# A long-convolution and expert kernel on one core: the filter's input laid out transposed and its constants loaded early, the experts' two turns joined, and the second to last stores issued from GpSimd's queue

## The chip, the cores and the metric

The kernel runs on 1 core of one Trainium2 chip. The metric is device time in microseconds (us) of one execution; lower is better. Before the change it was run three times: median 2395.51 us, from 2389.8 to 2403.55. One execution more was recorded by the hardware profiler; all trace times below are of that one and count from the start of its span. The engines are PE (matrix multiply; its weight loads are listed apart as PEld), ACT, DVE, POOL (GpSimd) and SP (which here only issues transfers).

## What is computed

Two layers follow each other. The first is a long convolution along the sequence (B = 4, S = 11456, D = 128) with a filter that a small network makes from position embeddings; the second sends each of the 45824 rows to one of E = 8 experts (F = 1024).

```python
h_filt = (np.maximum(pos_emb @ w1, 0.0) @ w2) * np.exp(-0.01 * pos)[:, None]
u = x * v
y = irfft(rfft(u, n=2*S) * rfft(h_filt, n=2*S))[:, :S]      # along the sequence
rows = (x * y).reshape(B * S, D)
...
logits = rows @ w_gate + modality_bias[modality_id]
e_idx = np.argmax(logits, axis=1)
gate_w = softmax(logits)[arange(N), e_idx]
for e in range(E):
    out[e_idx == e] = gate_w * (np.maximum(rows[e_idx == e] @ w1[e], 0.0) @ w2[e])
```

## The kernel before

**The convolution** is a two-stage transform of length 90 x 64, written as matrix products. An outer stage turns the sequence, in NQ = 16 parts, into the SBUF tile `A`, which has two blocks `A[:, 0]` and `A[:, 1]`; a middle stage works through `A` in NG = 30 groups of three rows; the inverse outer stage brings `A` back. The filter goes through the outer and the middle stage once, ahead of the four batches, and uses only `A[:, 0]`. Then every batch is transformed forward, multiplied with the filter's spectrum and transformed back; while a batch is transformed back, its rows are routed to the experts and the next batch is transformed forward.

**The filter's outer stage** (`filter_stages`) takes a part `q` through `load` (256 KB of position embeddings, on SP's queue), `turn` (four PE transposes, one ACT copy), `hidden` (four matmuls with `w1`, then one DVE operation that applies max and the window) and `transform` (four matmuls, two ACT copies into `A`). **Its middle stage** (`filter_middle`) takes a group `g` through `load` (192 KB of constants into a tile `b2`), `turn` (three transposes, an ACT copy `aT`), `spectrum` (three matmuls into `pz`; ACT and DVE split the result into a rounded half and a remainder, stacked as `z`) and `second` (four matmuls with `ws`, the split `w2`; ACT and DVE put the result into a tile `h`, from a ring of three, and POOL's queue stores it to the DRAM tensor `hs`, 384 KB a group).

**The order** on PE, ACT, DVE and SP is the order in which the code is written. Short tables (`FOUT`, `FMID`, `OUTER`, `LAST`, `MID`) give each stage's delay in steps; `steps` turns them into a list of steps, and `overlapped` lays the last F steps of one list over the first F of the next. `F1` lays the filter's middle over its outer stage; `F2` = 2 lays the first batch's forward stage (`load` of `x` and `v`, `product` on DVE, `transform` on PE) over the filter's last two steps. POOL's queue runs in program order too. Tiles named by `new_a` come from one pool of NA = 11 buffers, so that a load waits until the buffer that it is given has been read. A transfer waits besides for the one that was issued eight earlier through the same kind of queue.

**Routing.** For the last batch (`b == nb - 1`) the table `LAST` applies. Each of its NO = 8 parts `o` ends in `store` (the rows with their gate and token number, two transfers to `xr`) and `places` (their places, two transfers to `xi`), both on SP's queue. The very last part's `choice`, `store`, `send` and `places` are kept for `finale` and run inside the expert loop. `fetch` and `send_rows` read `xr` and `xi` back and scatter the rows, by indirect transfers from POOL's queue, into the expert-sorted tensor `xs`.

**The experts** (`experts`) run over 99 tiles of 512 rows, or 256 for the last ones. `rows_in(i)` loads a tile's rows (`x`, four buffers) on SP's queue, and for the first eight tiles their weights too; `rows_turn` transposes them (`px`) and splits them into `xh` and `xl`; `hidden` and `result` are three matmuls each per chunk `c` of 128 hidden units (eight chunks a tile), with `result` two chunks behind; after the last chunk ACT copies the sum to `oT`; `rows_out` transposes that (`pt`), DVE multiplies it by the gate into `ot`, and POOL's queue scatters the rows to `out`. In chunk 5 of a tile stands `rows_turn` of the next tile, in chunk 2 `rows_out` of the tile before.

Of the kernel before, what the change touches and what calls it, by code (L numbers as in the profile page):

```python
# [12 lines left out]
F32 = mybir.dt.float32  # L13
# [24 lines left out]
G = 3  # L38
# [21 lines left out]
FOUT = "load:0 transform:4 turn:1 hidden:2"  # L60
FMID = "turn:2 spectrum:3 second:5 load:1"
MID = "minus:2 turn:1 inverse:5 back:4 load_c:3 spectrum:2 load:0"
GD, OV, EA, MB, EM = 2, 2, 3, 1, 4
F1, F2, F3 = 1, 2, 1
# [113 lines left out]
def hyena_moe_kernel(ctx: ExitStack, tc: tile.TileContext, a: dict, out: bass.AP,  # L178
# [176 lines left out]
    with ExitStack() as cv:  # L355
# [22 lines left out]
        ws = keepp.tile([D, 2, D], F32R, name="ws")  # L378
# [24 lines left out]
        def split_constants():  # L403
            dve.tensor_copy(base, sm("reg"))
            dve.tensor_copy(both, small[:, SMALL["tri"][0]:SMALL["ones"][1]])

            act.copy(ws[:, 0], wf[:, 0])
            dve.tensor_sub(ws[:, 1], wf[:, 0], ws[:, 0].bitcast(F32))
# [78 lines left out]
        def filter_stages():  # L487
# [7 lines left out]
            def turn(q):  # L495
                t = kept.pop((q, "emb"))
                pT = bank("pT")
                for i in range(4):
                    pe.transpose(pT[:, D * i:D * i + D], t[:, D * i:D * i + D], ident)
                pTs = kept[q, 0] = new_a("pTs")[:, 0:512]  # L500
                act.copy(pTs, pT)

            def hidden(q):
                pTs = kept.pop((q, 0))
                m1 = bank("m1")
                for i in range(4):
                    pe.matmul(m1[:, D * i:D * i + D], pTs[:, D * i:D * i + D], wf[:, 1],
# [19 lines left out]
            todo = dict(turn=turn, hidden=hidden, transform=transform, load=load)  # L527
# [5 lines left out]

        def filter_middle():
# [4 lines left out]
            def load(g):  # L539
                t = kept[g, "b"] = new_a("b2")[0:2 * N2, 0:2 * GK].rearrange(  # L540
                    "p (j d) -> p j d", j=G)
                sp.dma_start(t, a["c_bc"][g, :, 0:2 * GK].rearrange("p (j d) -> p j d", j=G))

            def turn(g):
# [3 lines left out]
                aT = kept[g, "aT"] = new_a("aT")[0:2 * N2, 0:G * D]  # L548
                act.copy(aT, pa[0:2 * N2, 0:G * D])

            def spectrum(g):
                aT, b2 = kept.pop((g, "aT")), kept.pop((g, "b"))
                pz = bank("pz")
                zv = pz[:, 0:2 * GK].rearrange("p (m j) -> p m j", j=G)
                for j in range(G):
                    pe.matmul(zv[:, :, j], aT[:, D * j:D * j + D], b2[:, j],
                              start=True, stop=True)
                z = kept[g, "z"] = new_a("z", F32R)[:, 0:4 * GK].rearrange(
                    "p (b m) -> p b m", b=2)

                halves = slice(0, 64), slice(64, D)
                for blk, at in enumerate(halves):
                    act.copy(z[at, blk], pz[at, 0:2 * GK])
                for blk, at in enumerate(halves):
# [624 lines left out]
```

## Time and profile before

| of the profiled execution | |
|---|---|
| its time | 2370.12 us |
| its span, first to last instruction | 2367.9 us |
| granted PE clock, mean over the span | 0.977 |
| median of the three runs beside it | 2395.51 us |
| filter, outer stage: first PE instruction to first of the middle stage | 3.66 to 49.57 us |
| filter, middle stage, to the first product of batch 0 | 49.57 to 118.84 us |
| batch 0 forward, to the first transpose of its middle stage | 118.84 to 163.74 us |
| first expert row tile transposed | 1254.04 us |
| PE busy 1400 to 1500 | 97.27 us |

The times of the profile are read as stretches: which engine is busy in a stretch without a break, and, where it is not, what ended its wait. A row of the timeline has the start, the duration in us, the engine, the line, the operation with its output and inputs, the count of instructions that are merged in it, and in brackets the idle time before it with what ended it.

```profile
PE 2238.2 (95%) x14826; PEld 1874.1 (79%) x14826; DVE 1839.2 (78%) x3197; ACT 1515.7 (64%) x2969; POOL 994.7 (42%) x987
PEclk9999999999899999899998999999999999999999
DMA  3976667677867788575556722112221111111111
```

The first row has each engine's busy time and share of the span; the other two cut the span into 40 slices of 59 us and give, in tenths, the clock granted to PE and the busy share of the 16 transfer engines.

### The profile page before, as it was taken

The numbers are of one execution on the slowest core, as the hardware profiler recorded it, in microseconds if no ns is written. First come the engines' busy times: TensorE is split into PE (matmuls) and PEld (weight loads), VectorE is DVE, ScalarE is ACT, GpSimd is POOL, SyncE is SP. The second block draws the span as 40 slices with busy tenths as digits, with TensorE's granted clock in tenths as the row PEclk, the third lists the DMA queues.
The fourth block names the chain that finished last, engine by engine and source line by source line (L and its number), as shares of the span: only waits on it lengthen the run. The fifth ranks groups of instructions, "written<-read, shape, count | busy, mean of one in ns | idle before, by whom it ended". The sixth has DMA issues, their size and how long they took to land. (4 is left out here: it accounts for less than half of the span.)

```text
span 2367.9 us, 44124 instructions
## 1 busy us (share of the span) xinstructions
PE 2238.2 (95%) x14826; PEld 1874.1 (79%) x14826; DVE 1839.2 (78%) x3197; ACT 1515.7 (64%) x2969; POOL 994.7 (42%) x987
## 2 busy tenths in 40 slices
PE   8899999899989999899888999999999999999998
PEld 8789966798669966698446777777878888888898
DVE  3789888897788978797566777777777877777797
ACT  5757677577556766576445666666666666666676
POOL 0305400376435755276652554445444333333333
PEclk9999999999899999899998999999999999999999
DMA  3976667677867788575556722112221111111111
GB/s 114 314 298 197 220 223 223 185 226 260 288 209 227 225 285 298 183 222 174 174 163 184 246 68 72 61 62 74 67 62 60 59 46 45 45 46 46 39 41 34
DMA packets 188751, 359.04 MB, mean 152 GB/s; under 512 B 33937, under 2 KB 120285, under 8 KB 188521
## 3 DMA queue, kind: packets, MB, share of 16 engines
q1 hardware_dynamic: 161753, 296.77, 39.5%
q0 software_dynamic: 26608, 59.36, 7.4%
q8 instruction: 120, 1.97, 0.3%
q14 instruction: 110, 0.90, 0.1%
q10 hardware_dynamic: 160, 0.03, 0.0%
HBM read 271.63 MB, written 84.83 MB: 151 GB/s over the span
## 5 line engine op out<-in xcount | busy, mean ns | idle before, releaser
L1072 DVE SCALAR_TENSOR_TENSOR hl<-ph,hh 128x512 fp32r<-128x512 f32 x724 | 499.1, 689 | 249.7 <-ACT hh L1071 147.7
L1071 ACT ACTIVATE hh<-ph 128x512 fp32r<-128x512 f32 x724 | 434.0, 600 | 376.1 <-PE ph L1068 232.1
L1108 POOL DMA_INDIRECT out<-ot,idx x362 | 357.8, 988 | 651.3 <-DVE ot L1105 568.1
L264 POOL DMA_INDIRECT xs<-back,to x360 | 379.6, 1054 | 230.6 <-DVE y L701 81.3
L1066 PE MATMUL ph<-xh,wh 128*128 128x512 f32 (+1 forms) x792 | 304.0, 384 | 2.9 <-ACT wh L1037 2.9
L1089 PE MATMUL po<-hh,wh 128*128 128x512 f32 (+1 forms) x792 | 303.5, 383 | 0.0
L1068 PE MATMUL ph<-xl,wh 128*128 128x512 f32 (+1 forms) x792 | 295.7, 373 | 0.1
L1091 PE MATMUL po<-hl,wh 128*128 128x512 f32 (+1 forms) x792 | 294.9, 372 | 0.0
L1067 PE MATMUL ph<-xh,wl 128*128 128x512 f32 (+1 forms) x792 | 294.5, 372 | 0.0
L1090 PE MATMUL po<-hh,wl 128*128 128x512 f32 (+1 forms) x792 | 293.9, 371 | 0.0
L641 POOL TENSOR_TENSOR more<-more 128x384 f32<-128x384 f32 x112 | 112.4, 1004 | 278.0 <-DVE more L638 233.9
L647 DVE TENSOR_TENSOR part<-pz,rings 128x768 f32<-128x768 f32 x240 | 217.6, 948 | 0.0
L664 PE MATMUL pw<-rings,yT 128*128 128x128 f32 x1440 | 184.4, 279 | 5.4 <-DMA rings<-in_c_bc 5.4
L628 PE MATMUL pz<-rings,aT 128*128 128x128 f32 x1440 | 184.4, 279 | 3.9 <-ACT aT L616 2.3
L664 PEld LDWEIGHTS pw<-rings,yT 128*128 128x128 f32 x1440 | 174.4, 196 | 6.0 <-issue 6.0
L628 PEld LDWEIGHTS pz<-rings,aT 128*128 128x128 f32 x1440 | 174.3, 196 | 5.3 <-ACT aT L616 3.0
L687 PEld LDWEIGHTS wt<-ident,A 128*90 128x90 f32 x1024 | 124.1, 185 | 61.6 <-issue 26.2
L1068 PEld LDWEIGHTS ph<-xl,wh 128*128 128x128 f32 x792 | 149.5, 189 | 27.4 <-DVE xl L1053 0.3
L1091 PEld LDWEIGHTS po<-hl,wh 128*128 128x128 f32 x792 | 149.2, 188 | 27.0
L1066 PEld LDWEIGHTS ph<-xh,wh 128*128 128x128 f32 x792 | 149.7, 189 | 26.3 <-ACT wh L1037 3.3
L1067 PEld LDWEIGHTS ph<-xh,wl 128*128 128x128 f32 x792 | 150.0, 189 | 24.1 <-DVE wl L1038 0.4
L652 POOL TENSOR_TENSOR part<-part,more 128x384 f32<-128x384 f32 x112 | 122.2, 1091 | 110.0 <-DVE part L651 83.1
(186 smaller groups left out, 4426.9 us busy)
## 6 DMA issues: line engine op xcount, KB each, us to landing
seq<-in_x SPq DMA_DIRECT2D x128, 512.0 KB
rings<-in_c_bc SPq DMA_DIRECT2D x240, 192.0 KB
rings<-hs SPq DMA_DIRECT2D x120, 384.0 KB
seq<-in_v SPq DMA_DIRECT2D x64, 512.0 KB
xr<-xo SPq DMA_DIRECT2D x64, 365.6 KB
back<-xr SPq DMA_DIRECT2D x72, 325.0 KB
x<-xs SPq DMA_DIRECT2D x82, 260.0 KB
hs<-rings POOLq DMA_DIRECT2D x30, 384.0 KB
```

Source lines behind the costliest of these rows:

```text
L264: s = pool.indirect_dma_start(out=xs, out_offset=bass.IndirectOffsetOnAxis(ap=ix, axis=0), in_=src, in_offset=None, bounds_check=E * R - 1 ...
L628: pe.matmul(zv[:, blk, :, j], k["aT"][:, blk, D * j:D * j + D], k["b"][:, j, :], start=True, stop=True)
L664: pe.matmul(pw[:, 2 * N2 * j:2 * N2 * (j + 1)], k["yT"][:, blk, D * j:D * j + D], k["c"][:, j, :], start=True, stop=True)
L1066: pe.matmul(p, k[0, "h"][:, f:f + D], k["xh"], start=True, stop=False)
L1067: pe.matmul(p, k[0, "l"][:, f:f + D], k["xh"], start=False, stop=False)
L1068: pe.matmul(p, k[0, "h"][:, f:f + D], k["xl"], start=False, stop=True)
L1071: act.activation(hh, ph, AF.Relu)
L1072: dve.scalar_tensor_tensor(hl, ph, 0.0, hh.bitcast(F32), op0=ALU.max, op1=ALU.subtract)
L1089: pe.matmul(po, k[1, "h"][:, f], hh[:, t], start=g == 0, stop=False)
L1090: pe.matmul(po, k[1, "l"][:, f], hh[:, t], start=False, stop=False)
L1091: pe.matmul(po, k[1, "h"][:, f], hl[:, t], start=False, stop=g == NCH - 1)
L1108: s = pool.indirect_dma_start(out=out, out_offset=bass.IndirectOffsetOnAxis(ap=k["idx"][:, j:j + 1], axis=0), in_=ot[:, j, :], in_offset=N ...
```

## The change

Four things are changed.

1. The position embeddings are laid out transposed by the host, so that `turn` of the filter's outer stage is gone and `hidden` reads the loaded tile directly.
2. In the filter's middle stage the split is gone: `spectrum` ends in one ACT copy, `second` multiplies unsplit `w2` (float32) in two matmuls of 64 rows each, one on partitions 0 to 63 and one on 64 to 127, instead of four of 128 rows in float32r. `aT` and `z` are taken from the rings that the batches use later.
3. The group's constants go into `A[:, 1]`, which the filter doesn't use, and are issued one in each of the first 30 steps (`load_b`). `F2` = 18 and the table `FIRST` place batch 0's loads over the filter's last 18 steps, with its products and transforms 16 and 17 steps later.
4. For the last batch, `store` and `places` of part 6 are issued from POOL's queue instead of SP's. In the experts `rows_out` moves from chunk 2 to chunk 5, right behind `rows_turn`, and `result` ahead of both.

```diff
--- before.py
+++ after.py
@@ -57,11 +57,12 @@
 OUTER = ("turn0:1 turn1:1 lturn:3 biased:3 forward:2 load_x:0 product:1 half:2 choice:3 "
          "inverse:1 logits:2 send:4 load:0 store:4 places:5")
 LAST = ("inverse:2 turn0:1 half:3 lturn:4 biased:4 logits:3 turn1:1 choice:4 load_x:1 send:5 store:5 places:6")
-FOUT = "load:0 transform:4 turn:1 hidden:2"
-FMID = "turn:2 spectrum:3 second:5 load:1"
+FOUT = "load:0 hidden:2 transform:3"
+FMID = "turn:0 spectrum:1 second:3"
+FIRST = "forward:17 load:0 product:16"
 MID = "minus:2 turn:1 inverse:5 back:4 load_c:3 spectrum:2 load:0"
 GD, OV, EA, MB, EM = 2, 2, 3, 1, 4
-F1, F2, F3 = 1, 2, 1
+F1, F2, F3 = 1, 18, 1
 UNSURE = 5
 TG, FA, FB, FC = 20, 8, 14, 18
 NDYN = 8
...
@@ -375,7 +376,6 @@
-        ws = keepp.tile([D, 2, D], F32R, name="ws")
@@ -403,9 +403,6 @@
         def split_constants():
             dve.tensor_copy(base, sm("reg"))
             dve.tensor_copy(both, small[:, SMALL["tri"][0]:SMALL["ones"][1]])
-
-            act.copy(ws[:, 0], wf[:, 0])
-            dve.tensor_sub(ws[:, 1], wf[:, 0], ws[:, 0].bitcast(F32))
@@ -492,19 +489,11 @@
                 t = kept[q, "emb"] = new_a("emb")[:, 0:512]
                 sp.dma_start(t, a["pos_emb"][q])
 
-            def turn(q):
+            def hidden(q):
                 t = kept.pop((q, "emb"))
-                pT = bank("pT")
-                for i in range(4):
-                    pe.transpose(pT[:, D * i:D * i + D], t[:, D * i:D * i + D], ident)
-                pTs = kept[q, 0] = new_a("pTs")[:, 0:512]
-                act.copy(pTs, pT)
-
-            def hidden(q):
-                pTs = kept.pop((q, 0))
                 m1 = bank("m1")
                 for i in range(4):
-                    pe.matmul(m1[:, D * i:D * i + D], pTs[:, D * i:D * i + D], wf[:, 1],
+                    pe.matmul(m1[:, D * i:D * i + D], t[:, D * i:D * i + D], wf[:, 1],
                               start=True, stop=True)
                 r = new_a("r")[:, 0:512].rearrange("p (m f) -> p m f", m=8)
                 dve.scalar_tensor_tensor(
@@ -524,53 +513,50 @@
                     act.copy(A[:, 0].rearrange("p k c n -> p (k c) n")[:, :, n0:n0 + 2],
                              p[:, h, 0:4 * N1].rearrange("p (n k) -> p k n", n=2))
 
         def turn_back(g, blk, j):
 
             return A[:, blk, G * g + j].rearrange("p c n -> p (c n)")
 
+        def first_b(g):
+
+            return A[0:2 * N2, 1].rearrange("p (g j) c n -> p g j (c n)", j=G)[:, g]
+
+        def load_b(g):
+            sp.dma_start(first_b(g),
+                         a["c_bc"][g, :, 0:2 * GK].rearrange("p (j d) -> p j d", j=G))
+
         def filter_middle():
 
 
             kept = {}
-
-            def load(g):
-                t = kept[g, "b"] = new_a("b2")[0:2 * N2, 0:2 * GK].rearrange(
-                    "p (j d) -> p j d", j=G)
-                sp.dma_start(t, a["c_bc"][g, :, 0:2 * GK].rearrange("p (j d) -> p j d", j=G))
 
             def turn(g):
                 pa = bank("pa")
                 for j in range(G):
                     pe.transpose(pa[0:2 * N2, D * j:D * j + D], turn_back(g, 0, j), ident)
-                aT = kept[g, "aT"] = new_a("aT")[0:2 * N2, 0:G * D]
-                act.copy(aT, pa[0:2 * N2, 0:G * D])
+                aT = kept[g, "aT"] = ring("b")
+                act.copy(aT, pa[:, 0:G * D])
 
             def spectrum(g):
-                aT, b2 = kept.pop((g, "aT")), kept.pop((g, "b"))
+                aT, b2 = kept.pop((g, "aT")), first_b(g)
                 pz = bank("pz")
                 zv = pz[:, 0:2 * GK].rearrange("p (m j) -> p m j", j=G)
                 for j in range(G):
                     pe.matmul(zv[:, :, j], aT[:, D * j:D * j + D], b2[:, j],
                               start=True, stop=True)
-                z = kept[g, "z"] = new_a("z", F32R)[:, 0:4 * GK].rearrange(
-                    "p (b m) -> p b m", b=2)
-
-                halves = slice(0, 64), slice(64, D)
-                for blk, at in enumerate(halves):
-                    act.copy(z[at, blk], pz[at, 0:2 * GK])
-                for blk, at in enumerate(halves):
-                    dve.tensor_sub(z[halves[1 - blk], blk], pz[at, 0:2 * GK],
-                                   z[at, blk].bitcast(F32))
+                z = kept[g, "z"] = ring("c")
+                act.copy(z, pz[:, 0:2 * GK])
 
             def second(g):
+
                 z = kept.pop((g, "z"))
                 ph = pair("ph")
                 for m in range(2):
-                    pe.matmul(ph[:, m, 0:2 * GK], ws[:, 0], z[:, m], start=True, stop=False)
-                    pe.matmul(ph[:, m, 0:2 * GK], ws[:, 1], z[:, m], start=False, stop=True)
+                    at = slice(64 * m, 64 * m + 64)
+                    pe.matmul(ph[:, m, 0:2 * GK], wf[at, 0], z[at], start=True, stop=True)
                 v = ph[:, :, 0:2 * GK].rearrange("p m (c k) -> p m c k", c=2)
                 hf = ring("h")
                 h = hf.rearrange("p (m c k) -> p m c k", m=2, c=3)
@@ -580,7 +566,7 @@
                 pool.dma_start(hs[g].rearrange("p (m k) -> p m k", m=2),
                                h[:, :, 1:3].rearrange("p m c k -> p m (c k)"))
 
-            todo = dict(turn=turn, second=second, spectrum=spectrum, load=load)
+            todo = dict(turn=turn, second=second, spectrum=spectrum)
             return [(int(t), todo[n]) for n, t in (w.split(":") for w in FMID.split())]
 
         def middle_stages(b):
@@ -797,9 +783,10 @@
 
             def store(o):
                 xo = xo_of(b, o)
+                queue = pool if b == nb - 1 and o == NO - 2 else sp
                 for blk in range(2):
                     rows = xr[b].rearrange("(k n w m) r -> k n w m r", k=2, n=HALF, w=2)
-                    sp.dma_start(
+                    queue.dma_start(
                         rows[blk, :, :, 8 * o:8 * o + 8].rearrange("n w m r -> n w (m r)"),
                         xo[64 * blk:64 * blk + HALF].rearrange("p w s h r -> p w (s h r)"))
 
@@ -826,9 +813,10 @@
 
             def places(o):
                 ix = ix_t[(b * NO + o) % 2]
+                queue = pool if b == nb - 1 and o == NO - 2 else sp
                 for blk in range(2):
                     at = xi[b].rearrange("(k n w m) -> k n w m", k=2, n=HALF, w=2)
-                    sp.dma_start(
+                    queue.dma_start(
                         at[blk, :, :, 8 * o:8 * o + 8],
                         ix[64 * blk:64 * blk + HALF].rearrange("p (w m) -> p w m", w=2))
 
@@ -861,9 +849,9 @@
                     todo[name] = before_last(todo[name])
                 finale.extend([lambda: (choice(NO - 1), store(NO - 1)),
                                lambda: (send(NO - 1), places(NO - 1))])
-            table = [w.split(":") for w in (LAST if b == nb else OUTER).split()]
-
-            return steps(NQ, [(lambda q, t=int(t): min(q + t, NQ + 3) if b < nb else q + t, todo[n])
+            table = [w.split(":") for w in (LAST if b == nb else OUTER if b else FIRST).split()]
+
+            return steps(NQ, [(lambda q, t=int(t): min(q + t, NQ + 3) if 0 < b < nb else q + t, todo[n])
                               for n, t in table if n in todo])
 
         def early(first, second, n):
@@ -872,6 +860,8 @@
             return first[:at] + [second[0]] + first[at:] + second[1:]
 
         seq = overlapped(steps(NQ, filter_stages()), steps(NG, filter_middle()), F1)
+        for k in range(NG):
+            seq[k] = lambda f=seq[k], k=k: (f(), load_b(k))
         for b in range(nb + 1):
             if b > 0:
                 extra = ([lambda b=b: bias_load(b - 1)] + [lambda: None] * 2 + [bias_flag]
@@ -1132,10 +1122,9 @@
                 next(others, 0)
             if c < 4:
                 weights(i + 1, c)
+            result(at - 2)
             if c == (5 if i <= last and tiles[i][2] == T else 2):
                 rows_turn(i + 1)
-            result(at - 2)
-            if c == 2:
                 rows_out(i - 1)
 
 
@@ -1162,7 +1151,7 @@
 
     pos = spread(np.asarray(inputs["pos_emb"])).reshape(2, 64, 2, NQ, 4, -1)
     arrays["pos_emb"] = np.ascontiguousarray(
-        pos.transpose(3, 2, 1, 4, 0, 5).reshape(NQ, D, -1))
+        pos.transpose(3, 0, 5, 4, 2, 1).reshape(NQ, D, -1))
     ids = np.asarray(inputs["moe_modality_id"]).astype(np.int64, copy=False).reshape(B, S)
     arrays["moe_modality_id"] = np.ascontiguousarray(np.stack([
         spread(a).reshape(D, 2, NO, 2, 4).transpose(0, 2, 4, 1, 3).reshape(D, NO * NC)
```

**PE, from the filter's outer to its middle stage.** `s1` are the outer matmuls of `transform`, `pa` the transposes, `pz` the `spectrum` products, `ph` those of `second`. Before:

```order
L507 MATMUL m1_489<-wf_119,pTs_473 128x128 x4
L520 MATMUL s1_496<-bs2_118,r_480 128x180 x4
L520 MATMUL s1_503<-bs2_118,r_494 128x180 x4
L547 MATMUL pa_512<-ident_72,A_115 128x128 x3
L547 MATMUL pa_520<-ident_72,A_115 128x128 x3
L556 MATMUL pz_526<-b2_510,aT_516 128x128 x3
L547 MATMUL pa_537<-ident_72,A_115 128x128 x3
L556 MATMUL pz_543<-b2_518,aT_524 128x128 x3
L547 MATMUL pa_554<-ident_72,A_115 128x128 x3
L556 MATMUL pz_560<-b2_535,aT_541 128x128 x3
L572 MATMUL ph_569<-z_530,ws_120 128x384
L573 MATMUL ph_569<-z_530,ws_120 128x384
```

The same place now:

```order
L496 MATMUL m1_391<-wf_119,emb_359 128x128 x4
L509 MATMUL s1_398<-bs2_118,r_381 128x180 x4
L509 MATMUL s1_406<-bs2_118,r_396 128x180 x4
L539 MATMUL pa_413<-ident_72,A_115 128x128 x3
L539 MATMUL pa_419<-ident_72,A_115 128x128 x3
L548 MATMUL pz_424<-A_115,rings_114 128x128 x3
L539 MATMUL pa_430<-ident_72,A_115 128x128 x3
L548 MATMUL pz_435<-A_115,rings_114 128x128 x3
L539 MATMUL pa_441<-ident_72,A_115 128x128 x3
L548 MATMUL pz_446<-A_115,rings_114 128x128 x3
L559 MATMUL ph_451<-rings_114,wf_119 128x384 x2
```

`hidden` (m1) reads `emb` instead of the transposed copy `pTs`, the constants are read from `A`, and a group has one row of two `ph` matmuls where it had two pairs (its second pair follows the last row shown before).

**SP's queue, from the last batch's routing to the first expert tile.** `xr` and `xi` are the stored rows and places, `x`, `w1r` and `w2r` the first tile's rows and weights. Before:

```order
L802 DMA xr3_61<-xo2_85 90x1x1040 x2
L831 DMA xi3_65<-ix1_87 90x1x8 x2
L802 DMA xr3_61<-xo0_83 90x1x1040 x2
L831 DMA xi3_65<-ix0_86 90x1x8 x2
L992 TENSOR_LOAD tab1_98
L995 ISA
L995 DMA x_14737<-xs_66 128x520
L1003 TENSOR_LOAD tab1_98
L1007 ISA
L1007 DMA w1r_14742<-in_moe_w1 128x1024
```

The same place now:

```order
L789 DMA xr3_61<-xo2_85 90x1x1040 x2
L819 DMA xi3_65<-ix1_87 90x1x8 x2
L982 TENSOR_LOAD tab1_98
L985 ISA
L985 DMA x_14382<-xs_66 128x520
L993 TENSOR_LOAD tab1_98
L997 ISA
L997 DMA w1r_14387<-in_moe_w1 128x1024
```

The four transfers of part 6 (`xo0`, `ix0`) are gone from between part 5's and the first tile's; on POOL's queue they now stand behind the third batch's scatters and ahead of the first tile's scatter to `out`.

**PE in a tile of the experts.** `ph` and `po` are the sums of `hidden` and `result`. Before, around `rows_out` in chunk 2 (`px` stood three chunks later, by itself):

```order
L1089 MATMUL po_19322<-hh_19277,wh_19170 128x512
L1090 MATMUL po_19322<-hh_19277,wl_19171 128x512
L1091 MATMUL po_19322<-hl_19278,wh_19170 128x512
L1103 MATMUL pt_19326<-ident_72,oT_19308 128x128 x4
L1066 MATMUL ph_19345<-xh_19239,wh_19137 128x512
```

Now, around both turns in chunk 5:

```order
L1079 MATMUL po_18967<-hh_18975,wh_18815 128x512
L1080 MATMUL po_18967<-hh_18975,wl_18816 128x512
L1081 MATMUL po_18967<-hl_18976,wh_18815 128x512
L1039 MATMUL px_19012<-ident_72,x_18768 128x128 x4
L1093 MATMUL pt_19021<-ident_72,oT_18953 128x128 x4
L1056 MATMUL ph_19040<-xh_18868,wh_18782 128x512
```

The transposes of `oT` moved three chunks back and stand behind those of the next tile's rows.

More of the change, by code (lines that the diff above doesn't have):

```diff
@@ L525, in transform @@
                              p[:, h, 0:4 * N1].rearrange("p (n k) -> p k n", n=2))
-            todo = dict(turn=turn, hidden=hidden, transform=transform, load=load)
+            todo = dict(hidden=hidden, transform=transform, load=load)
             return [(int(t), todo[n]) for n, t in (w.split(":") for w in FOUT.split())]
```

## The prediction

> **What bounds the kernel now.** The page's busy shares name PE, and the 40 slices put its holes at three places: the start, the slice around 112 us, the slice around 1250 us. From there I read the timeline of each stage, first the filter's outer stage on PE's weight loads (start, duration, engine, line, operation, count; in brackets the idle time ahead and what ended it).
>
> ```profile
> 6.69 2.04 PE L507 MATMUL m<-wf,pTs 128*128 128x128 f32 x8 [1.10 <-DMA wf<-in_w]
> 9.38 1.54 PE L507 MATMUL m<-wf,pTs 128*128 128x128 f32 x8
> 14.38 0.51 PEld L499 LDWEIGHTS pT<-ident,emb 128*128 128x128 f32 x4
> 14.86 0.97 PEld L507 LDWEIGHTS m<-wf,pTs 128*128 128x128 f32 x8
> 15.75 1.22 PEld L520 LDWEIGHTS s<-bs,r 128*128 128x128 f32 x8
> 16.93 0.51 PEld L499 LDWEIGHTS pT<-ident,emb 128*128 128x128 f32 x4
> 49.57 0.88 PE L547 MATMUL pa<-ident,A 128*128 128x128 f32 x6 [0.91 <-ACT A L524]
> ```
>
> No gap: a part costs 16.93 - 14.38 = 2.55 us of PE, namely transposes 0.48, `hidden` 0.89, `transform` 1.18. PE bounds this stage. A float32 matmul stands as two records, so the 1.18 us are four of 180 columns, 1.64 ns a column. The first `hidden` waits for the weights `wf` until 6.69 and runs at half speed (2.04 us).
>
> Next the middle stage: two steady groups on PE, then ACT's copy of `ph` with what ended its idle time (us, times), then how the stage ends.
>
> ```profile
> 89.42 0.44 PE L572 MATMUL ph<-z,ws 128*128 128x384 f32 x1
> 90.22 0.49 PE L547 MATMUL pa<-ident,A 128*128 128x128 f32 x3
> 90.55 0.83 PE L556 MATMUL pz<-b,aT 128*128 128x128 f32 x6
> 91.23 0.44 PE L572 MATMUL ph<-z,ws 128*128 128x384 f32 x1
> L577 ACT COPY rings<-ph x30: 478/479/483, 55.4 to 117.8; 128x384 f32<-128x384 f32 x30
>   DMA hs<-rings: 13.3, 12
> 117.80 0.48 ACT L577 COPY rings<-ph 128x384 f32<-128x384 f32 x1 [2.76 <-DMA hs<-rings]
> 100.00:120.00 20.00, 10.22 (x60) 8.31 (x58) 12.10 (x28) 8.74 (x21) 5.80 (x9) 0.82 0.99 365
> ```
>
> Undisturbed, a group takes 91.23 - 89.42 = 1.81 us: `second` 0.80, transposes 0.33, `spectrum` 0.68. But the 30 copies stretch over 62.4 us, 2.15 each: 13.3 us of ACT's idle ended with a store from the ring of three `h`. The worst is the last copy (2.76): in the last row (us; busy time of PE, PEld, DVE, ACT, POOL; clock; DMA share; GB/s) the transfer engines are full (0.99, by batch 0's loads) and PE works half the time. So the stores of the last groups and the loads of the next stage collide.
>
> **Filter, outer stage.** Without the transposes a part costs 2.55 - 0.48 = 2.07 us. Sixteen parts save 7.7 us. Against that, the first `hidden` still waits for `wf` at 6.69, so what stood ahead of it saves nothing (part 0's transposes, some of part 1's), and the clock comes up later: the first two `hidden` cost 2.04 and 1.54 instead of 0.89, and now more of the work falls into the slow time. I take 7.7 - 2.2 = 5.5 us, with 4 and 7 as bounds: the middle begins at 44.0. The copy `pTs` goes from ACT, which isn't late here.
>
> The slow stretch ends near 10.4 in the trace, some 7 us after PE's first transposes. The Trainium skill, page "TensorE: Matmul & The Clock Gate", section "What's actually happening", says that the clock is halved until about one window of 3.4 us was busy; without transposes the busy time begins at 6.69, so by that rule the clock rises between 10.1 and 13.5. An estimate from that page: up to 1.7 us less gain than without the rule. The sum goes by the 5.5 above.
>
> **Filter, middle stage.** Transposes and `spectrum` stay, 1.01 us. `second` becomes two float32 matmuls of 384 columns, 64 rows each: 384 x 1.64 ns = 0.63 us apiece. Whether two halves of the array run side by side is shown best by the only other 64-row work, in the inverse stage, and by the work behind it.
>
> ```profile
> 300.91 1.86 PEld L471 LDWEIGHTS s<-fwd,seq 64*128 64x128 f32 x32
> 302.86 0.76 PEld L744 LDWEIGHTS xT<-ident,xo 109*128 109x128 f32 x8
> L547 PEld LDWEIGHTS pa<-ident,A 128*128 128x128 f32 x75 | 9.7, 140 | 0.9
> ```
>
> These 32 records are 16 matmuls of 90 columns: at 1.64 ns, one after the other, 2.36 us. They take 302.86 - 300.91 = 1.95, so they overlap at least partly; each has a short weight load of 61 ns, which 384 columns would hide. Ends: 0.63 (side by side) and 1.26 us (serial). I take 0.63, since 1.95 rules out serial and its load pace explains the rest. After the last load 0.09 us pass (302.77 to 302.86) before the full-height load; I charge that twice a group, plus one transpose load (140 ns) that nothing hides: 0.32, bounds 0 and 0.4. A group: 1.01 + 0.63 + 0.32 = 1.96 us. Thirty: 59 us; with 0.6 for the last copy and its handover to DVE the first product stands at 44.0 + 59.0 + 0.6 = 103.6.
>
> The Trainium skill, page "TensorEngine Tiling (Array Packing)", section "Key Properties", speaks against this edit: "Changing tiling mode (not just tile) drains the TensorE". It gives no price. By the rule each group pays two drains; the 0.09 us gap agrees with it. If there were none the group would be 1.64.
>
> Does the ring of `h` bind instead? A tile is taken for copy, DVE and landing.
>
> ```profile
> 85.84 0.48 ACT L577 COPY rings<-ph 128x384 f32<-128x384 f32 x1 [0.68 <-DMA hs<-rings]
> 87.51 0.67 POOL L580 DMA_DIRECT2D hs<-rings  x1 [1.30 <-DVE rings L579]
> 91.04 0.48 ACT L577 COPY rings<-ph 128x384 f32<-128x384 f32 x1
> ```
>
> From the copy at 85.84 to the same tile's next at 91.04, with no wait ahead of it, are 5.2 us: the ring can turn in 1.73 us a group, below 1.96. It binds only while loads run too. Those are now issued behind the embeddings and the constants, in the steps from 18 before the end. The pool of 11 lets 5.5 parts of `x` and `v` ahead (5.8 MB); at the 365 GB/s above that takes 16 us, from about 31 to 47-51, around the middle's first stores. I take 0 to 5 us of disturbance inside the range. Later loads are released by products and come behind the stores. Constants in `A[:, 1]` cost nothing more than before: the same 192 KB a group, earlier.
>
> ```profile
> 118.84 1.22 DVE L452 TENSOR_TENSOR seq<-seq 128x1024 f32<-128x1024 f32 x1
> 121.30 1.22 DVE L452 TENSOR_TENSOR seq<-seq 128x1024 f32<-128x1024 f32 x1
> 163.74 1.53 PE L615 MATMUL aT<-ident,A 128*128 128x128 f32 x12 [0.85 <-ACT A L482]
> ```
>
> Before, the first product stood at 118.84: outer and middle together save **15.2 us**. Batch 0's forward stage then goes 2.46 us a part on DVE, as before, since sixteen parts on DVE cost more than their loads; it keeps its 44.9 us.
>
> **The stores from POOL's queue.** SP's queue around the change of stages (`xr` stores, `xi` places, then the first tile's rows `x`), and the first tile on PE:
>
> ```profile
> 1237.06 1.73 SPq L831 DMA_DIRECT2D xi<-ix  x2
> 1244.52 1.71 SPq L802 DMA_DIRECT2D xr<-xo  x2
> 1245.54 0.90 PE L761 MATMUL lt<-ident,lT 128*109 128x128 f32 x4 [0.28 <-ACT lT L755]
> 1246.71 3.12 SPq L831 DMA_DIRECT2D xi<-ix  x2
> 1251.25 0.36 SPq L995 DMA_DIRECT2D x<-xs  x1
> 1254.04 1.08 PE L1049 MATMUL px<-ident,x 128*128 128x128 f32 x4 [7.60 <-DMA x<-xs]
> 1258.02 0.79 PE L1066 MATMUL ph<-xh,wh 128*128 128x512 f32 x1 [2.89 <-ACT wh L1037]
> ```
>
> The rows' load (1251.25) stands behind part 6's transfers; SP was free at 1238.8. Without them it goes out about 1240.5 and lands 2.8 us later, about 1243.3. What is late next is PE's own work: `lt` ends at 1246.4. Then `px`, and the chain that took 1258.02 - 1254.04 = 4.0 us shrinks to 2.4 because the weights are no longer what comes last (2.89 us idle by them): first matmul 1248.8, **9.2 us** earlier. Bounds 6 (weights still last) and 12. On POOL's queue the stores stand behind batch 3's scatters and ahead of the first `out` scatter, due over ten us later: nothing waits there.
>
> **The experts' joined turns.** PE's transposes `pt` of `oT` wait for ACT (who waited for the copy, us and times), and one such place:
>
> ```profile
>   PEld pt L1103: 28.2, 36
>   PE pt L1103: 15.3, 15
> 1496.60 0.39 PE L1091 MATMUL po<-hl,wh 128*128 128x512 f32 x1
> 1496.93 0.59 ACT L1094 COPY oT<-po 128x512 f32<-128x512 f32 x1
> 1497.57 0.66 PE L1103 MATMUL pt<-ident,oT 128*128 128x128 f32 x4 [0.58 <-ACT oT L1094]
> ```
>
> PE lost 15.3 us in 15 tiles; its weight loads were late in 36 (28.2). Three chunks later (one is 1.36 us, 4.1 in all) the copy at 1496.93 has long ended. The transposes and the matmuls stay as many. I take **18 us**, PE's idle and a fifth of the weight loads' remainder; bounds 5, if ACT's lateness shows at the next `result` instead, and 21.
>
> A tile's buffer comes free 4.1 us later, since `ot` reads it too:
>
> ```profile
> 1499.26 0.68 DVE L1105 TENSOR_TENSOR ot<-pt,x 128x512 f32<-128x512 f32 x1
> 1499.97 12.22 SPq L995 DMA_DIRECT2D x<-xs  x2
> 1501.50 0.60 PE L1049 MATMUL px<-ident,x 128*128 128x128 f32 x4
> 1513.41 0.60 PE L1049 MATMUL px<-ident,x 128*128 128x128 f32 x4
> ```
>
> The load released at 1499.97 is for a tile turned two steps of 11.9 us after 1501.50, at about 1525.3: 25 us ahead, now 21, and it lands in 2.8. Costed at nothing; cover 18 us.
>
> **Sum.** 15.2 + 9.2 + 18.0 = 42.4 us off the profiled execution's own 2370.12: 2327.7. That execution is 25 us (1.07%) below the median of the runs; scaled by 2395.51 / 2370.12 = 1.0107, **2353 us**.
>
> **Rivals.**
> - *The 64-row halves don't run side by side.* Serial, `second` costs 0.63 more, 30 x 0.63 = 19 us; 2353 + 19 = 2372. For it: the 90-column row shows only part of an overlap. Against: 1.95 is less than 2.36.
> - *ACT's lateness moves.* The copy waits no more but `result` two chunks behind does: the experts save 3 instead of 18, 2368. For it: ACT is as busy as before. Against: two chunks are 2.7 us, more than the copy's delay.
> - *The rows' load waits for something else* (the last scatters into `xs`, an earlier transfer), so that the moved stores give 1 instead of 9: 2361.
> - *Two of these together*: 2380 to 2387, about no change.
> - *Slower: the rows of a tile come late.* Their buffer now comes free 4.1 us later. If a load took over 21 us instead of 2.8, each further us would be paid once a round of the four buffers, some 25 times. It decides from 21 + 42 / 25 = 22.7 us; at 25 us it is 4 x 25 = 100 us against 42 saved, 58 slower, times 1.0107: 2454. The row `x<-xs` that lands within 2.8 us speaks against it.
>
> **How the numbers follow.** Forecast 0.68, serial halves 0.10, moved lateness 0.10, stores 0.05, two together 0.04, slower 0.03. The forecast's own range is 2338 to 2367: terms between 11 and 18 (filter), 6 and 12 (stores), 12 and 21 (experts). For 8 in 10 I reach to the single rivals and to both ends of the ring and clock: 2330 to 2380. A measurement of this kernel can tell about 0.5%, 12 us: faster by more 0.93, within 0.04, slower 0.03.
>
> **What would show it.** Right: first middle transpose near 44, groups of 1.96 us on PE, first product near 103.6 with no `hs` wait over 1 us ahead of it; `px` of the first tile near 1231 (15.2 earlier by the filter, 7.6 by the stores), right behind `lt`; no idle ahead of `pt`. Wrong: `second` of 1.3 us a group; waits for `hs` at 50-60; `result` waiting for DVE's `hl` in the experts; waits for `x<-xs` at `px`.

## The result, and the profile after

| | before | after |
|---|---|---|
| median of four runs | 2392.66 us (2386.92 to 2403.55) | 2336.48 us (2328.46 to 2345.48) |
| the profiled execution | 2370.12 | 2328.46 |
| first transpose of the filter's middle stage | 49.57 | 42.97 |
| first product of batch 0 | 118.84 | 103.37 |
| first transpose of batch 0's middle stage | 163.74 | 147.54 |
| first expert matmul | 1258.02 | 1231.32 |
| last PE instruction | 2358.05 | 2316.50 |

The changed kernel is faster: the ratio of the runs is 0.976, with a 95% interval from 0.9723 to 0.9798, some 57 us. (The four runs of the changed kernel include its profiled execution, their fastest; the four of before don't include theirs, which is 17 us below their fastest.) The two profiled executions are 41.7 us apart, and that is what the traces can divide up: 16.2 us by batch 0's middle stage, 10.5 from there to the first expert matmul, 14.9 from that to the last PE instruction (the experts). Rows of PE are compared by their starts, here and in what follows.

The filter on PE, from the timeline of the changed kernel (columns as before): its first `hidden`, two steady parts, the change to the middle stage and one steady group there.

```profile
6.32 3.62 PE L496 MATMUL m<-wf,emb 128*128 128x128 f32 x16 [6.32 <-DMA wf<-in_w]
9.78 1.39 PE L509 MATMUL s<-bs,r 128*128 128x180 f32 x8
11.00 1.05 PE L496 MATMUL m<-wf,emb 128*128 128x128 f32 x8
13.12 1.05 PE L496 MATMUL m<-wf,emb 128*128 128x128 f32 x8
42.97 0.85 PE L539 MATMUL pa<-ident,A 128*128 128x128 f32 x6 [1.00 <-ACT A L513]
46.92 0.92 PE L559 MATMUL ph<-rings,wf 64*128 64x384 f32 x4
47.77 0.55 PE L539 MATMUL pa<-ident,A 128*128 128x128 f32 x3
48.15 0.83 PE L548 MATMUL pz<-A,rings 128*128 128x128 f32 x6
48.91 0.92 PE L559 MATMUL ph<-rings,wf 64*128 64x384 f32 x4
```

A part of the outer stage takes 13.12 - 11.00 = 2.12 us. A group takes 48.91 - 46.92 = 1.99 us. The four records of `ph` (two float32 matmuls of 384 columns) are over in 0.92 us; one after the other they would need 1.26.

What ACT's copy of `ph` waited for in the changed kernel (us, times), and the first product on DVE:

```profile
L563 ACT COPY rings<-ph x30: 478/478/478, 47.9 to 104.3; 128x384 f32<-128x384 f32 x30
  DMA hs<-rings: 2.4, 3
103.37 1.21 DVE L449 TENSOR_TENSOR seq<-seq 128x1024 f32<-128x1024 f32 x1
```

The stores' share of that waiting fell from 13.3 to 2.4 us, and the 30 copies now stretch over 56.4 instead of 62.4 us.

SP's queue and PE between the last batch and the experts:

```profile
1220.27 1.73 SPq L819 DMA_DIRECT2D xi<-ix  x2
1223.38 0.37 SPq L985 DMA_DIRECT2D x<-xs  x1
1229.01 0.69 PE L747 MATMUL lt<-ident,lT 128*109 128x128 f32 x4 [0.38 <-ACT lT L741]
1229.53 0.60 PE L1039 MATMUL px<-ident,x 128*128 128x128 f32 x4
1231.32 0.53 PE L1056 MATMUL ph<-xh,wh 128*128 128x512 f32 x1 [1.19 <-ACT wh L1027]
```

The first rows' load goes out 3 us after part 5's places, and `px` stands right behind `lt`, with no wait. From the start of the last `lt` matmul to that of the first expert matmul were 11.85 us, now 1.90.

In the experts, who waited for ACT's copy to `oT`, and PE's waits ahead of `result` in that stage (us in total, times, longest):

```profile
  PEld pt L1093: 1.3, 1
  PE pt L1093: 1.0, 1
PE po L1079 <- ACT hh L1061: 2.3, 1, 2.3
...
PE po L1081 <- DVE hl L1062: 1.4, 2, 1.2
```

The idle time ahead of `pt` is gone (15.3 to 1.0 us), and hardly any of it shows at `result`.

### The profile page after: what moved, and what is told of

The parts are those of the page before. It is cut to its first block, busy times and chain, and to the rows that moved or that the text cites. A ratio compares the mean times of both kernels' runs of the same rounds, so it can differ in the third digit from the quotient of the medians.

```text
span 2326.5 us, 43809 instructions
## 1 busy us (share of the span) xinstructions
PE 2223.6 (96%) x14762; PEld 1855.0 (80%) x14762; DVE 1806.5 (78%) x3136; ACT 1500.7 (65%) x2922; POOL 1002.7 (43%) x991
## 3 DMA queue, kind: packets, MB, share of 16 engines
q8 instruction: 119, 1.95, 0.3%
## 5 line engine op out<-in xcount | busy, mean ns | idle before, releaser
L1079 PE MATMUL po<-hh,wh 128*128 128x512 f32 (+1 forms) x792 | 294.6, 372 | 2.4 <-ACT hh L1061 2.3
L1079 PEld LDWEIGHTS po<-hh,wh 128*128 128x128 f32 x792 | 149.4, 189 | 29.7 <-ACT hh L1061 4.1
L1080 PEld LDWEIGHTS po<-hh,wl 128*128 128x128 f32 x792 | 149.4, 189 | 26.1
```

What stands on the lines that cost most here:

```text
L1079: pe.matmul(po, k[1, "h"][:, f], hh[:, t], start=g == 0, stop=False)
L1080: pe.matmul(po, k[1, "l"][:, f], hh[:, t], start=False, stop=False)
```

## The experiments

The twelve runs were made in three sets of four. The same kernel before had medians of 2368.10, 2308.19 and 2312.21 us in them, and 2392.66 in the comparison above; so ratios are compared only within a set, and stages across sets only where the text says so. The stages of the twelve profiles, by the trace: first transpose of the filter's middle stage, first product, first transpose of batch 0's middle stage, from the last `lt` to the first expert matmul, and from that to the last PE instruction ("experts").

| run | ratio (95%) | middle | product | batch 0 | `lt` to matmul | experts |
|---|---|---|---|---|---|---|
| e1_filter | 0.9935 (0.9911-0.9959) | 43.73 | 104.12 | 148.29 | 11.32 | 1105.66 |
| e2_stores | 0.9971 (0.9946-0.9996) | 49.52 | 119.90 | 164.42 | 1.90 | 1105.28 |
| e3_turns | 0.9931 (0.9906-0.9956) | 49.64 | 118.88 | 163.89 | 12.37 | 1085.59 |
| e4_before_again | 0.9974 (0.9942-1.0005) | 49.99 | 119.34 | 162.94 | 11.86 | 1095.62 |
| e5_after_again | 0.9883 (0.9864-0.9901) | 42.74 | 104.37 | 148.55 | 1.90 | 1075.62 |
| e6_late_loads | 0.9898 (0.9882-0.9913) | 43.75 | 106.17 | 150.95 | 1.90 | 1076.22 |
| e7_same_rows | one run | 44.50 | 123.18 | 167.36 | | 1112.22 |
| e8_out_in_2 | 0.9905 (0.9890-0.9921) | 44.26 | 104.68 | 148.87 | 1.90 | 1079.49 |
| e9_before_twice | 1.0160 (1.0142-1.0178) | 48.81 | 119.62 | 163.60 | 11.59 | 1119.46 |
| e10_after_twice | 0.9886 (0.9866-0.9906) | 42.86 | 104.28 | 148.45 | 1.90 | 1077.62 |
| e11_before_chip | 1.0002 (0.9990-1.0015) | 49.93 | 119.81 | 164.62 | 11.59 | 1078.65 |
| e12_pairs_warm | 0.9858 (0.9840-0.9876) | 42.02 | 103.70 | 148.68 | 4.47 | 1076.98 |

### The three parts, each alone on the kernel before

**e1_filter** is the changed kernel with the two edits of part 4 undone: stores and places of part 6 on SP, `rows_out` in chunk 2.

```diff
-                queue = pool if b == nb - 1 and o == NO - 2 else sp
...
-            result(at - 2)
             if c == (5 if i <= last and tiles[i][2] == T else 2):
                 rows_turn(i + 1)
+            result(at - 2)
+            if c == 2:
                 rows_out(i - 1)
```

> Only the filter's part (parts 1 to 3 of the change) on the kernel before. Theory (the three parts are apart and add up): the middle stage begins near 43, the first product near 103.4, and the trace saves 16 us by the first transpose of batch 0's middle stage; between that and the first expert matmul, and in the experts, nothing changes (within 2 us). Ratio 0.993 of before. Rival A (before's collision of stores and loads varies and costs its plain runs some 15 us more than its profiled one): the ratio shows 30 us, 0.987. Rival B (the filter's gain makes the later stages wait): less than 10 us, 0.996.

**e2_stores** is the kernel before with those `queue` lines alone.

```diff
+                queue = pool if b == nb - 1 and o == NO - 2 else sp
...
-                    sp.dma_start(
+                    queue.dma_start(
```

> Only part 6's stores and places on POOL's queue. Theory: the first rows load goes out 10 us earlier, the first expert matmul comes 9 to 10.5 us earlier, ratio 0.996. Rival (the first rows' load waits for something else then): the first matmul comes less than 3 us earlier, ratio 0.999.

**e3_turns** is the kernel before with the order of the turns alone.

```diff
-            if c == (5 if i <= last and tiles[i][2] == T else 2):
-                rows_turn(i + 1)
             result(at - 2)
-            if c == 2:
+            if c == (5 if i <= last and tiles[i][2] == T else 2):
+                rows_turn(i + 1)
                 rows_out(i - 1)
```

> Only the joined turns in the experts. Theory: from the first expert matmul to the last PE instruction 14 to 18 us less, PE idle ahead of pt under 2 us in all, ratio 0.993. Rival (the earlier result of the order was needed, ACT's lateness shows at result): result waits for hh and hl by over 8 us in all, ratio 0.997 or more.

**e4_before_again** is the kernel before, unedited.

> The kernel before itself, unchanged. If its first profiled execution was only a quick one of a scattered lot, the new profile lies within its plain runs (2385 to 2400) and the extra 15 to 25 us are spread over the stages with the granted clock or sit in a named stage; if a profiled execution is quicker than a plain one as such, it is again near 2370, with plain runs near 2392. Ratio 1.000 either way; it shows how wide an interval no change gives.

Each edit moved its own columns of the table; the experts scatter by 10 us besides, with nothing changed in them. The filter: batch 0's middle stage begins at 148.29 instead of 162.94 to 164.42, and the ratio is the one expected; rival A's 0.987 lies outside the interval, rival B's 0.996 at its edge. The stores: 1.90 instead of 11.3 to 12.4 us, which is 9.4 to 10.5 less, as expected; the interval of the ratio holds both 0.996 and 0.999, so the trace decides here. The turns: 1085.59 us of experts, against 1095.62 to 1105.66 in the three others; `pt` didn't wait at all and `result` 3.8 us for `hh` and `hl`, so that the rival is out. The ratios multiply to 0.9838, 38.4 us of 2368. The kernel before, against itself, came out at 0.9974 in the same set: a single ratio here is uncertain by a quarter of a per cent. The level of the runs had moved, from 2387 to 2404 us in the first comparison to 2346 to 2382 for e4, so neither branch of its expectation came as written; but e4's profiled execution (2362.24 us) lies in the middle of its plain runs. A profiled execution isn't quicker as such, and 2370.12, 17 us under the fastest plain run beside it, was a quick one.

### The changed kernel again, and parts of it taken back

**e5_after_again** is the changed kernel, unedited.

> The changed kernel itself. Theory (the parts add up, and the 57 us of the first comparison held some scatter of its few runs): ratio 0.9837, the product of the three single parts, that is 38 us. Rival (the parts help each other by some 16 us): ratio 0.976 again.

It was neither: 0.9883, 28 us by the medians (1.2%). Filter (148.55) and stores (1.90) are as they were; what shrank is found below.

**e6_late_loads** puts batch 0's loads into the filter's last two steps.

```diff
-F1, F2, F3 = 1, 18, 1
+F1, F2, F3 = 1, 2, 1
...
-            table = [w.split(":") for w in (LAST if b == nb else OUTER if b else FIRST).split()]
+            table = [w.split(":") for w in (LAST if b == nb else OUTER).split()]
```

> The changed kernel with batch 0's loads laid over the filter's last 2 steps, as before, in place of 18. Theory (the early loads are needed, since stores and loads collide at the end of the filter): first product 108 to 115 instead of 102.8, first transpose of batch 0's middle stage 154 to 160 instead of 147.5. Rival (layout and fewer matmuls give it all): within 2 us of the changed kernel at both places.

The expectation failed: the first product came 1.8 us later, not 5 to 12. SP's queue in the kernel before, in this run and in the changed kernel, the constants (in the first two) and the first load of `x`:

```profile
39.06 61.69 SPq L542 DMA_DIRECT2D b<-in_c_bc  x30
103.34 0.33 SPq L447 DMA_DIRECT2D seq<-in_x  x1
```

```profile
28.03 7.65 SPq L528 DMA_DIRECT2D A<-in_c_bc  x15
35.94 0.33 SPq L444 DMA_DIRECT2D seq<-in_x  x1
```

```profile
35.17 0.33 SPq L444 DMA_DIRECT2D seq<-in_x  x1
```

The loads go out at 35 to 36 us wherever the table puts them. Before, the 30 constants held SP's queue from 39.06 to 100.75, since each waits for a buffer out of the pool of 11; with the constants in `A[:, 1]` the last 15 are through in 7.65 us, and batch 0's first loads follow. So the constants' new place is what made the loads early, as far as the queue shows; no run moves the constants alone, and `pTs`, `aT` and `z` left the pool of 11 too. The table is worth about 2 us.

**e7_same_rows** lets both matmuls of `second` use rows 0 to 63.

```diff
-                    at = slice(64 * m, 64 * m + 64)
+                    at = slice(0, 64)
```

> The changed kernel, but both matmuls of second read rows 0 to 63, so that they can't run side by side; half of the filter's spectrum is computed from the wrong rows. Theory (side by side is what makes the group 1.99 us, and PE bounds the stage): a group takes 2.6 us, the first product comes 19 us later, at 122. Rival (something else sets the 1.99 us): less than 5 us later.

```profile
61.60 1.55 PE L559 MATMUL ph<-rings,wf 64*128 64x384 f32 x4
63.09 0.55 PE L539 MATMUL pa<-ident,A 128*128 128x128 f32 x3
64.23 1.55 PE L559 MATMUL ph<-rings,wf 64*128 64x384 f32 x4
```

Its groups on PE take 64.23 - 61.60 = 2.63 us, and the first product came at 123.18, 18.8 us after e5's. On different rows the two run side by side, and PE bounds this stage. (With the other spectrum the rows go to other experts, so its later stages aren't compared.)

**e8_out_in_2** puts `rows_out` back into chunk 2 and leaves the rest.

```diff
             if c == (5 if i <= last and tiles[i][2] == T else 2):
                 rows_turn(i + 1)
+            if c == 2:
                 rows_out(i - 1)
```

> The changed kernel with rows_out back in chunk 2; result stays ahead of rows_turn. Theory (pt waited for ACT's oT because it stood too early): experts 1096 to 1106 us from first matmul to last PE instruction instead of 1085, pt idle 15 to 23 us, ratio to before 0.990. Rival (it is result's place ahead of rows_turn): experts under 1090.

The expectation failed: 1079.49 us of experts, only 3.9 over e5 (the ratio, 0.9905, is near the 0.990 expected, but so is e5's 0.9883), and `pt` waited hardly at all:

```profile
  PEld pt L1093: 2.0, 2
  PE pt L1093: 1.4, 2
```

That left two readings: `result`'s place ahead of `rows_turn`, or ACT being less late in this set. The traces spoke for the second. In the kernel before, ACT around the late `oT` that the prediction shows, and the matmul that feeds the second row:

```profile
1494.12 0.61 ACT L1037 CAST wh<-w1a 128x512 fp32r x1
1494.56 0.39 PE L1068 MATMUL ph<-xl,wh 128*128 128x512 f32 x1
1495.93 0.60 ACT L1071 ACTIVATE hh<-ph 128x512 fp32r<-128x512 f32 x1 [1.20 <-PE po L1091]
```

The input of `hh` was there at 1494.95 and ACT was free, yet it began at 1495.93. Starts of `hh` over 0.4 us later than the last matmul into `ph` and ACT's previous instruction (of 724): 20 in the first profile of before, 14 to 38 in the first set, 37 in the first profile of after; none in e5, e6 and e8. The last set tests what such lateness costs, and shows before without it.

### ACT's lateness by itself

**e9_before_twice** and **e10_after_twice** are the kernel before and the changed one with ACT's copy doubled.

```diff
                 act.copy(k["oT"][:, 0:n], po)
+                act.copy(k["oT"][:, 0:n], po)
```

> The kernel before with ACT's copy of oT done twice, so that oT is ready 0.5 us later in each of 99 tiles. Theory (pt, which stands right behind, has no slack for a late ACT, so every delay of ACT there is paid): the experts get 35 to 50 us longer, and PE idles ahead of pt in most tiles. Rival (only rare long pauses show): under 10 us longer.

> The changed kernel with the same doubled copy. Theory (three chunks, 4.1 us, cover it): experts longer by under 5 us than without it, no idle ahead of pt. Rival (ACT's lateness only moves to the next result): 20 us or more, with idle ahead of po that ends by hh or hl.

**e11_before_chip** is the kernel before, unedited.

> The kernel before, for the profile on this chip. The chips differ: pauses of ACT (hh starting over 0.4 us later than its input) were 22 to 47 an execution on one chip and 0 or 1 on another. Theory: the idle ahead of pt follows them; with 20 or more pauses the experts take 1095 to 1106 us and pt waits 15 to 23 us, with none 1080 us and under 3 us.

Who waited for `oT`, in e9, then in e10:

```profile
L1095 ACT COPY oT<-po x99: 372/586/586, 1230.4 to 2331.3; 128x512 f32<-128x512 f32 x82, 128x256 f32<-128x256 f32 x17
  PEld pt L1104: 57.9, 83
  PE pt L1104: 23.4, 82
```

```profile
  PEld pt L1094: 1.3, 2
  PE pt L1094: 0.9, 1
```

Half a microsecond of ACT cost the kernel before 1119.46 - 1078.65 = 40.8 us, and the changed one 2.0 (1077.62 against e5's 1075.62, of the set ahead). Both expectations held, and since ACT has the same extra work in both kernels, it is not that work itself that costs. In chunk 2 `pt` has no slack; in chunk 5 it has enough. And e11, the kernel before without a late start of `hh`, needs 1078.65 us for the experts instead of 1100.04: `pt` waits 1.4 us there. So that side of its theory held; the other, 20 pauses or more, is what the earlier profiles show from which it was drawn. Its premise, that the chips differ, isn't borne out: the record gives chip number 6 for the first set, with its pauses, and for this one, and 5 for the second. (Whether number 6 was the same chip both times isn't on record.)

### Two edits more on the changed kernel

**e12_pairs_warm** runs `second` for two groups at once and lets PE transpose the identity until `wf` is there.

```diff
-FMID = "turn:0 spectrum:1 second:3"
+FMID = "turn:0 spectrum:1 second:2"
...
+                if q == 0:
+                    w1 = bank("w1")
+                    for i in range(28):
+                        pe.transpose(w1[:, D * (i % 4):D * (i % 4) + D], ident, ident)
...
             def second(g):
-
-                z = kept.pop((g, "z"))
-                ph = pair("ph")
-                for m in range(2):
-                    at = slice(64 * m, 64 * m + 64)
-                    pe.matmul(ph[:, m, 0:2 * GK], wf[at, 0], z[at], start=True, stop=True)
+                if g % 2 == 0:
+                    return
+                phs = []
+                for k in (g - 1, g):
+                    z = kept.pop((k, "z"))
+                    ph = pair("ph")
+                    phs.append((k, ph))
+                    for m in range(2):
+                        at = slice(64 * m, 64 * m + 64)
+                        pe.matmul(ph[:, m, 0:2 * GK], wf[at, 0], z[at], start=True, stop=True)
```

> The changed kernel with second run for two groups at a time, so that PE goes to 64 rows and back half as often, and 28 transposes of the identity ahead of the first hidden, so that PE is busy before wf lands. Theory: the change of height costs 0.31 us a group, so the middle stage up to the first product takes 4.6 us less than 59.9 (55.3); the first hidden runs at full rate (0.9 us instead of 1.8) and the middle stage begins 1.5 to 2 us earlier than 43. Ratio to the kernel before 0.003 under that of the change. Rivals: the height change costs nothing (59.9), the clock comes up at the same time as without the transposes (43).

```profile
2.52 4.62 PE L497 MATMUL w<-ident 128*128 128x128 f32 x28 [2.52 <-POOL ident masks.py:199]
6.97 1.95 PE L500 MATMUL m<-wf,emb 128*128 128x128 f32 x16
55.10 0.48 ACT L572 COPY rings<-ph 128x384 f32<-128x384 f32 x1 [4.03 <-DMA hs<-rings]
60.01 0.55 PE L543 MATMUL pa<-ident,A 128*128 128x128 f32 x3
63.64 0.55 PE L543 MATMUL pa<-ident,A 128*128 128x128 f32 x3
```

Both steps are seen, and neither pays as expected. Two groups take 63.64 - 60.01 = 3.63 us, 1.82 each instead of 1.99: half the changes of height save 0.17 a group. But two results at once fill the ring of `h` while batch 0's loads still run, and ACT's waits for stores, 7.5 us in all with one of 4.03, take the gain back: 61.7 us to the first product, like e5's 61.6, instead of 55.3. The first two `hidden` took 1.95 us instead of 3.62. But the 28 transposes were too many and held PE until 6.97, so the middle began 0.7 us before e5's instead of 1.5 to 2. Its ratio's interval overlaps that of e5 and of e10, and in its profile, which is of its slowest run (2291.45 us; the others took 2278.28 to 2283.20), the stages are hardly shorter; as a better version it isn't shown. (Its 4.47 us to the first expert matmul are a wait for the first weights, in this one execution.)

## Why the prediction held, point by point

- **Outer stage.** 5.5 us were forecast, 6.6 measured in the first pair (49.57 to 42.97), 4 to 7 being the bounds. The slow clock cost some 1.7 us (the first two `hidden` took 3.62 us, at full speed in e12 1.95), within the 2.2 taken off; besides, `wf` came at 6.32 instead of 6.69. The Trainium skill, page "TensorE: Matmul & The Clock Gate", section "What's actually happening", had the clock rise after about one busy window of 3.4 us; from 6.32 that is 9.7, and the row at 9.78 is the first at full speed. In e12 PE was busy from 2.52, by the single records it was at full speed from 5.33, and the row at 6.97 ran so. The traces agree with the page within 0.6 us.
- **Middle stage.** The group of 1.96 us measured 1.99, the first product forecast for 103.6 came at 103.37. That it is so close is partly luck: the stage began 1.0 us earlier than forecast and took 0.8 longer. Side by side was right (e7), and so was 0.32 us for two changes of height: e12 saves 0.17 a group by half of them, which makes 0.34. The Trainium skill, page "TensorEngine Tiling (Array Packing)", section "Key Properties", has a change of the tiling mode drain the TensorE. The trace agrees that a change costs time, about a third of `second`'s 0.98 us (1.99 - 1.01); that it is a drain no run here shows.
- **Early loads.** The loads were early, as forecast (35 us instead of the 31 reckoned), but not by the steps. "Those are now issued behind the embeddings and the constants, in the steps from 18 before the end": the steps are worth about 2 us (e6); what frees the queue is, as far as it shows, the constants' place. "Constants in `A[:, 1]` cost nothing more than before" left out that they also gain.
- **Stores.** 9.2 us forecast; 11.3 to 12.4 us became 1.90 in six traces (4.47 in e12, whose first weights came late), so 9.4 to 10.5. `px` does stand right behind `lt`.
- **Joined turns.** The mechanism was right: PE waited for ACT's `oT`, and three chunks cover it (e9, e10). The size, "I take 18 us", was that of one execution. It measured 14.9 in the first pair and 10 to 20 in the first set, in executions with 14 to 38 late starts of `hh`; where there were none it is 3.0 (e11 to e5, across two sets). The size was read from an execution with such pauses, and the executions compared had them too: that was luck. No rival came true: in the changed kernel `result` waits 3.7 us in all for `hh` and `hl`, not 15, and no tile's rows came late.
- **Sum.** 42.4 us forecast, 41.7 between the profiled executions; that is luck in part, since the filter gave 16.2 instead of 15.2, the stretch with the stores 10.5 instead of 9.2 and the experts 14.9 instead of 18, and these cancel. The median, forecast at 2353, was 2336.48: just under the forecast's own range from 2338 to 2367, inside 2330 to 2380. The runs gave 57 us, then 28 in the second set. The smaller gain is the turns without pauses. For the 15 us more in the first comparison the traces have no place: its runs of before lie 17 to 33 us over their own profiled execution, those of the changed kernel only 4 to 17 over theirs, so the scaling by 1.0107 is the term that didn't carry over. With four runs a side and levels that differ by 3.6% for one kernel it wasn't followed further, and stays open.

## What to carry over

An engine's idle time in one trace is the price of another engine's lateness in that execution alone: the same wait was 15.3 us here and 1.4 in e11. Ask how much slack the waiting instruction has, and test it by delaying the other engine on purpose, as the doubled copy does. SP's queue, which runs in program order, came free when what it waited for was gone; moving the loads up in the table added about 2 us. And the 64-row pair of matmuls was worth its two changes of height here: side by side saved 0.64 us a group (e7), the changes cost about 0.34 (e12).

## What was not expected of the hardware

The same kernel took 2308 to 2393 us (medians) in different sets, its granted clock between 0.97 and 0.99. Part of it are late starts on ACT of 0.4 to 2.4 us (20 of them with 19.9 us in all in the first profile) that no view gives a cause for; all but one lie ahead of 1800 us, while POOL still scatters the last batch's rows into `xs`. None came in the later sets. They aren't ACT's alone. The profile calls it "issue" where an engine was idle and waited for nothing that it shows; one such row, of PE in the changed kernel between 150 and 1190 us (us in all, times, longest):

```profile
PE pl L738 <- issue: 11.2, 6, 5.2
```

From batch 0's middle stage to the experts, PE was idle for 14 to 20 us in this way in each profile of the first comparison and the first set, and for 0.2 us at most in the later ones; its whole idle time there was 69 to 80 us against 49 to 55. That is a part of what the batch stages vary by: from batch 0's middle stage to the first expert matmul the kernel before took 1094 and 1092 us in its first profile and in e4, 1060 in e11; the changed one 1084, then 1046 in e5. What makes the difference between the sets wasn't found; the expectation of e11 took it for the chip, which the chip's number doesn't bear out.
